# A second expert unit's first layer as seven block products instead of 32 plain ones, with the sums and counts around it moved

## The chip, the cores and the metric

The kernel runs on one core of one Trainium2 chip. The metric is the device time of one execution in microseconds (us). Three runs of the kernel before the change took 675.66, 675.84 and 678.24 us, median 675.84. One execution was profiled; it took 678.39 us, of which its instructions span 676.7 us.

The engines are named as in the profile: PE (matrix multiplication, with PEld for its weight loads), DVE (vector), ACT (scalar), POOL (GpSimd) and SP (the queue that issues most transfers). Each engine runs its own list of instructions strictly in order, and waits on semaphores for what other engines and transfers have not yet delivered.

## The reference

```python
# 1. attention, B=8, H=8, S=576, head_dim 64: causal, with a bias from a running sum of relu(s)
scores = scale * q @ k.T + minimum(-(cum_i - cum_j), 0)      # masked above the diagonal
x = softmax(scores) @ v                                      # -> x: (8, 576, 512)
# 2. a mixture of experts on x: E=8 experts, D=512, F=1024
logits = x @ w_gate
local_gate = sigmoid(x @ w_local)
e = argmax(logits) if s == 0 or local_gate < 0.5 else e of the token before
p = softmax(logits)
out = p[e] * (relu(x @ w1[e]) @ w2[e])                       # one expert per token, all float32
```

## The kernel before, in words

**Attention, then experts.** The attention runs batch by batch for the first 200 us. The tokens are routed in four groups of two batches: DVE finds each token's expert and its row in a table in memory, and POOL scatters the rows of `x` into this table (`put` in the class `Router`, L367 a memset and L370 an indirect transfer; 18 scatters a group, then 8 that store padding). The last group's routing and scatters overlap with the experts.

**Units.** The experts' work is cut into units, one letter each in `ORDER` (L66). Nearly all are whole units: up to 256 tokens of one expert. A unit has two layers: `x @ w1` with relu, and `h @ w2` with the gate. The phases alternate: (1,0), (1,1), (2,0), (1,2), (2,1), (1,3), (2,2) and so on, where (1,u) is the first layer of unit u and (2,u) its second. PE runs them in this order without a break between them.

**Plain and block layers.** A letter P in `ORDER` has a plain first layer (`layer1`, L864): 8 chunks of 4 products of 128x128 by 128x256, each of which the chip runs as two matmuls, so 64 matmuls. ACT alone turns the result into `hT` with a relu (L866). A letter D has its first layer, and both letters have their second layer, as seven block products in place of eight (`layer_split`, Winograd's form of Strassen's scheme): the tokens' matrix and the weights are each cut into 2x2 blocks, a11 to a22 and b11 to b22. Before the products come sums: `row_sums` makes s1 = a21+a22, s2 = s1-a11 and a21 = a11-a21 (L703 to L705), `row_fourth` a12 = a12-s2 (L709), and `weight_first` to `weight_fourth` make t1 = b12-b11, t2 = b22-t1, b12 = b22-b12 and b21 = b21-t2 (all L654). The order of the products is

- product 1 (a11, b11), copied by ACT to `sa`; product 2 (a12, b21), added to it by DVE as c11; then the fourth weight sum and the fourth row sum;
- product 6 (s2, t2), product 7 (a21, b12), product 5 (s1, t1), product 4 (a22, b21 after its sum), product 3 (a12 after its sum, b22).

After each, DVE adds the product to the partial sums (L762: c11, sb, sa, sb again and c22, c21, c12), and ACT applies the relu (L770) or the gate (L766). In the first layer a product is 16 matmuls of 128x128 by 128x128 (L730), in the second 8 of 128x128 by 128x256 (L737).

**Who does the sums.** DVE does all weight sums and, for the first five units, the row sums of `xT`; POOL does the row sums of `hT` for all units. The row sums of `hT` of unit 0 stand at the start of phase (1,1), those of unit 1 at the third step of (2,0).

**What sets the order.** The order is written out by hand. A layer calls `at(i)` after its i-th step; a table `todo`, filled by `plan` and `job`, says what is issued there on the other engines. `at` also takes the next waiting scatter, and lets it wait for the latest ACT instruction so far (`self.relu`): the scatters are spread over the steps, one a step. A plain layer has eight steps and a block layer seven. After all scatters and paddings are out, the rows of unit 5 and its `w1` may be loaded.

**Whole units assigned.** `assign_doubles` (its rows run from L387 to L465) computes with 26 small DVE instructions which expert and which rows the units 5 and later have. It needs the counts of the last group (`late_rows`, planned at step 2 of phase (1,1)).

## Time and profile before

| | |
|---|---|
| runs | 675.66, 675.84, 678.24 us; median 675.84 |
| profiled execution | 678.39 us, span 676.7 us, clock 0.996 |
| PE busy | 661.4 us (98%) |
| DVE busy | 492.9 us (73%) |
| POOL busy | 369.5 us (55%) |
| ACT busy | 195.5 us (29%) |
| phase (1,0), plain | from 200.46 us, with 1.5 us of routing in it |
| phase (2,0) starts | 230.37 us |
| phases (1,2), (2,1), (1,3), (2,2), (1,4) start | 242.45, 255.60, 267.69, 280.19, 292.28 us |

The shares are averages over the attention and the experts. Around the change, between 215 and 295 us, they are others, so the reader should look at stretches of time. In the timeline a row has the start in us, the length in us, the engine, line, operation, output and inputs, shapes, how many instructions are merged, and in brackets the idle time before and what ended it.

### The profile page before, as it was taken

Reading aid. Unit: us, or ns where it says so; the run is one execution under the profiler, and the core shown is the slowest. Engines: PE = TensorE matmul, PEld = TensorE weight load, DVE = VectorE, ACT = ScalarE, POOL = GpSimd, SP = SyncE. Lnnn points to the kernel's source line nnn. Section 1 sums busy time; section 2 is a strip of 40 time slices with the busy share of each in tenths; the row PEclk is TensorE's granted clock in tenths of the full one; section 3 lists DMA queues with packets and bytes.
Section 4 is the critical chain, followed back from the end, with each engine's and each line's share of the span. In section 5 each row is a group of like instructions: output and inputs, shape, how many; then the busy total and the mean of one; then the engine's idle time right before and its main releaser. Section 6 shows DMA issues by size and latency. Waiting matters only on the chain.

```text
span 676.7 us, 18439 instructions
## 1 busy us (share of the span) xinstructions
PE 661.4 (98%) x7501; PEld 571.4 (84%) x7501; DVE 492.9 (73%) x942; ACT 195.5 (29%) x353; POOL 369.5 (55%) x525
## 2 busy tenths in 40 slices
PE   8999999999999999999999999999999999999995
PEld 6888787888878899999999999999589687796884
DVE  4565857987966899978988988955467664766843
ACT  4454635546332112122122121212111121111111
POOL 3562377777645878955556557540642543714733
PEclk9999999999999999999999999999999999999998
DMA  7665575677549798489967455616939785933002
GB/s 263 193 176 167 177 219 177 213 228 245 181 129 398 227 341 266 191 275 346 349 262 254 182 188 187 253 44 248 353 58 392 277 364 130 291 144 115 25 15 76
DMA packets 56549, 145.75 MB, mean 215 GB/s; under 512 B 13104, under 2 KB 33968, under 8 KB 51464
## 3 DMA queue, kind: packets, MB, share of 16 engines
q1 hardware_dynamic: 47352, 124.23, 55.6%
q0 software_dynamic: 9008, 20.11, 8.3%
q8 instruction: 61, 1.00, 0.6%
q14 instruction: 32, 0.26, 0.1%
q10 hardware_dynamic: 96, 0.15, 0.1%
HBM read 123.83 MB, written 20.85 MB: 214 GB/s over the span
## 4 chain that ended last, share of the span: by engine, by line
PE 84%; DVE 7%; issue 4%; POOL 2%; DMA 1%; ACT 0%; SPq 0%; POOLq 0%; DVEq 0%
PE p L730 26%; PE p L737 25%; PE ps L1217 10%; PE po L1274 6%; PE pb L1274 6%; PE hp L864 3%; PE yp L887 2%; PE hp L855 2%; PE lp L237 1%; PE ph L1235 1%; POOL out_dram L839 1%; DVE wt L654 1%; PE po L1287 1%; DVE w2b L654 1%; PE pb L1287 1%
## 5 line engine op out<-in xcount | busy, mean ns | idle before, releaser
L737 PE MATMUL p<-w2b,hT 128*128 128x256 f32 (+1 forms) x720 | 163.0, 379 | 0.0
L737 PEld LDWEIGHTS p<-w2b,hT 128*128 128x128 f32 (+1 forms) x720 | 133.3, 187 | 21.9 <-PE hp L855 1.6
L730 PE MATMUL p<-xTs,w1b 128*128 128x128 f32 (+1 forms) x1040 | 142.9, 295 | 0.0
L730 PEld LDWEIGHTS p<-xTs,w1b 128*128 128x128 f32 x1040 | 137.9, 191 | 3.6 <-issue 1.6
L1218 ACT ACTIVATE e<-ps 128x768 f32<-128x768 f32 (+1 forms) x96 | 76.6, 885 | 60.9 <-PE ps L1217 60.8
L839 POOL DMA_INDIRECT out_dram<-y,gi x37 | 47.0, 1270 | 74.0 <-ACT y L766 66.2
L766 ACT ACTIVATE y<-y,gi 128x256 f32<-128x256 f32 (+1 forms) x71 | 34.5, 505 | 161.5 <-DVE y L762 161.5
L770 ACT ACTIVATE hT<-hT 128x512 f32<-128x512 f32 (+1 forms) x52 | 36.8, 711 | 143.8 <-DVE hT L762 143.8
L1217 PE MATMUL ps<-qb,kb 64*128 64x384 f32 (+4 forms) x516 | 76.8, 442 | 0.5 <-DVE xb L1297 0.4
L1217 PEld LDWEIGHTS ps<-qb,kb 64*128 64x128 f32 x516 | 47.5, 187 | 27.4 <-ACT e L1218 9.7
L370 POOL DMA_INDIRECT table<-xb,idx x54 | 56.8, 1052 | 14.2 <-issue 12.8
L737 PE MATMUL p<-wt,hSs 128*128 128x256 f32 (+1 forms) x272 | 63.3, 379 | 0.0
L709 POOL TENSOR_TENSOR hT<-hT,hSs 128x512 f32<-128x512 f32 (+1 forms) x14 | 21.1, 1506 | 76.8 <-PE p L737 76.7
L1201 POOL TENSOR_SCALAR_AFFINE_SELECT e<-e 128x128 f32<-128x128 f32 (+1 forms) x96 | 37.4, 406 | 41.8 <-ACT e L1218 41.0
L730 PE MATMUL p<-xSs,wt 128*128 128x128 f32 (+1 forms) x416 | 58.9, 295 | 0.4 <-DVE wt L654 0.4
L737 PEld LDWEIGHTS p<-wt,hSs 128*128 128x128 f32 (+1 forms) x272 | 50.7, 186 | 8.0
L730 PEld LDWEIGHTS p<-xSs,wt 128*128 128x128 f32 x416 | 55.6, 192 | 1.1 <-PE p L730 0.6
L762 DVE TENSOR_TENSOR hT<-p,sa 128x512 f32<-128x512 f32 (+1 forms) x48 | 31.2, 667 | 32.7 <-PE p L730 32.7
L1274 PE MATMUL pb<-vg,e 128*64 128x66 f32 x1280 | 41.4, 222 | 2.0 <-issue 1.9
L1274 PE MATMUL po<-vg,e 128*64 128x66 f32 x1280 | 41.4, 223 | 1.8 <-issue 1.8
L1274 PEld LDWEIGHTS pb<-vg,e 128*64 128x64 f32 x1280 | 39.4, 138 | 2.7 <-issue 2.6
L1274 PEld LDWEIGHTS po<-vg,e 128*64 128x64 f32 x1280 | 38.9, 138 | 3.3 <-issue 2.1
(304 smaller groups left out, 952.5 us busy)
## 6 DMA issues: line engine op xcount, KB each, us to landing
w2b<-in_w_dram SPq DMA_DIRECT2D x20, 2048.0 KB
w1b<-in_w_dram SPq DMA_DIRECT2D x19, 2048.0 KB
va<-in_v_dram SPq DMA_DIRECT2D x32, 320.0 KB
xq<-table SPq DMA_DIRECT2D x72, 130.0 KB
kb<-in_k_dram SPq DMA_DIRECT2D x31, 288.0 KB
qb<-in_q_dram SPq DMA_DIRECT2D x31, 288.0 KB
w1b<-in_w_dram SPq DMA_DIRECT2D x4, 512.0 KB
table<-xb,idx POOLq DMA_INDIRECT x54
```

The source lines that it names most:

```text
L370: put = self.nc.gpsimd.indirect_dma_start(out=self.halves, in_=src, element_offset=0, in_offset=None, out_offset=bass.IndirectOffsetOnAxis ...
L709: self.adder(u, layer).tensor_tensor(a12, a12, (self.xS, self.hS)[layer][u][1], op=Alu.subtract)
L730: mm(ps[:, m * h : m * h + h], lhsT=b[:, k, (c * of + m) * P : (c * of + m) * P + P], rhs=a[:, k, :], start=m == 0 and k == 0, stop=m == o ...
L737: mm(ps[:p, c * w : c * w + w], lhsT=a[:, k, c * p : c * p + p], rhs=b[:, k, :], start=c == 0 and k == 0, stop=c == parts - 1 and k == n - 1)
L762: nc.vector.tensor_tensor(to[:, c], part, s[:, c], op=Alu.add)
L766: ins = nc.scalar.mul(to[:, c], to[:, c], gi[:p, parts * r + c, 1:2]).ins
L770: return gated(to, r) if layer else nc.scalar.activation(to, to, Act.Relu).ins
L839: put = nc.gpsimd.indirect_dma_start(out=out, out_offset=bass.IndirectOffsetOnAxis(ap=idx, axis=0), in_=y, element_offset=0, bounds_check= ...
L1201: nc.gpsimd.affine_select(out=ap, in_=ap, compare_op=Alu.is_ge, fill=0.0, base=base, pattern=n, channel_multiplier=-1)
L1217: mm(ps[:, h, at : at + z - a], lhsT=kb[d, key : key + P], rhs=qb[d, a:z], start=True, stop=True)
L1218: exps[n, u] = nc.scalar.activation(e[:, :, : WIDTH[u]], ps, Act.Exp, scale=scale).ins
L1274: of = mm(po[part][d, j - a, :], lhsT=weights_of(n, c, j, h), rhs=vgs[n % NV][:, c if j < 2 * G1 else G1 + c, h, :], start=(first and i == ...
```

## The change

Unit 1 becomes a D: its first layer runs as seven block products. Its row sums of `x` and its three first weight sums are issued in phase (1,0), at steps 3 to 6. Phase (1,1) thereby has seven steps in place of eight. The three sums of the first unit's `w2` are issued one at each of steps 4, 5 and 6 of phase (1,1), ahead of the additions of that step's next product, where before they stood at its end. `assign_doubles` is no longer run at step 5 of phase (1,1): it is a generator with one more stop, taken piece by piece at steps 2 and 4 of (1,2), steps 1, 3 and 4 of (2,1), and step 0 of (1,3).

```diff
-ORDER = "PPDDDDDDDDXTXDMXD"
+ORDER = "PDDDDDDDDDXTXDMXD"
...
         v.tensor_scalar(x, x, float(REST_MIN), None, Alu.is_ge)
+        yield
         v.tensor_tensor(x, x, self.used, op=Alu.add)
...
-        plan(1, 1, 5, lambda: list(router.assign_doubles()))
+        doubles = router.assign_doubles()
+        for place in ((1, 2, 2), (1, 2, 4), (2, 1, 1), (2, 1, 3), (2, 1, 4), (1, 3, 0)):
+            plan(*place, lambda: next(doubles, None))
...
                     if u == 0:
-                        places = (1, 1, 6), (1, 1, 7), (1, 1, 7)
+                        places = (1, 1, 4), (1, 1, 5), (1, 1, 6)
...
-                    job(2, u - 2, 1 if self.kind(u - 2) in "DX" else "pre" if u > 2 else 3, self.row_sums, u, 0)
+                    elif u == 1:
+                        places = (1, 0, 4), (1, 0, 5), (1, 0, 6)
+                    if u == 1:
+                        job(1, 0, 3, self.row_sums, u, 0)
+                    else:
+                        job(2, u - 2, 1 if self.kind(u - 2) in "DX" else "pre" if u > 2 else 3, self.row_sums, u, 0)
```

Lines of the class `Experts` stand one further down in the changed kernel (L655 for L654, L763 for L762, L704 to L706 for L703 to L705).

On DVE, in phases (1,0) and (1,1), the scan `incl` that ends the last group's routing was followed at once by the group's rows (`at` and on):

```order
L314 SCALAR_TENSOR_TENSOR incl<-seg,hot 128x152
L331 TENSOR_TENSOR at<-pos,base 128x144
L333 TENSOR_TENSOR base<-base,pos 128x8
L334 TENSOR_TENSOR at<-at,hot 128x144
L336 TENSOR_REDUCE row<-at 128x18
```

Now there stand in the same place, from `incl` to the first row of the group:

```order
L314 SCALAR_TENSOR_TENSOR incl<-seg,hot 128x152
L704 TENSOR_TENSOR xSs<-xTs 128x256
L705 TENSOR_TENSOR xSs<-xSs,xTs 128x256
L706 TENSOR_TENSOR xTs<-xTs 128x2x128
L655 TENSOR_TENSOR wt_4100<-w1b 128x1024
L655 TENSOR_TENSOR wt_4100<-w1b,wt_4100 128x1024
L655 TENSOR_TENSOR w1b<-w1b 128x2x512
L763 TENSOR_TENSOR hT<-p_4167,sa 128x4x128
L655 TENSOR_TENSOR w1b<-w1b,wt_4100 128x2x512
L710 TENSOR_TENSOR xTs<-xTs,xSs 128x2x128
L763 TENSOR_TENSOR sb<-p_4187,sa 128x512
L331 TENSOR_TENSOR at<-pos,base 128x144
```

The row sums, weight sums and first additions of unit 1 have come ahead of the group's rows.

The next place on DVE is the end of phase (1,1) and the start of unit 0's second layer, (2,0). Before, `assign_doubles` ended there, and the sums of unit 0's `w2` followed it:

```order
L433 TENSOR_SCALAR bused<-bused 128x8
L434 TENSOR_TENSOR bused<-bused,n_f 128x8
L465 TENSOR_TENSOR a0used<-a0used,bused 128x8
L654 TENSOR_TENSOR wt_4269<-w2b 128x1024
L654 TENSOR_TENSOR wt_4269<-w2b,wt_4269 128x1024
L654 TENSOR_TENSOR w2b<-w2b 128x4x256
L762 TENSOR_TENSOR y<-p_4298,sa 128x256
```

Now the other additions of unit 1's first layer stand between the end of the group's rows (`pad_i`) and that place, with the sums of unit 0's `w2` among them:

```order
L381 TENSOR_SCALAR pad_i<-pad_at,half 128x8
L763 TENSOR_TENSOR sa<-p_4226,sb 128x512
L763 TENSOR_TENSOR sb<-p_4239,sb 128x512
L763 TENSOR_TENSOR hT<-p_4239,sa 128x4x128
L655 TENSOR_TENSOR wt_4251<-w2b 128x1024
L763 TENSOR_TENSOR hT<-p_4255,sa 128x4x128
L655 TENSOR_TENSOR wt_4251<-w2b,wt_4251 128x1024
L763 TENSOR_TENSOR hT<-p_4269,sb 128x4x128
L655 TENSOR_TENSOR w2b<-w2b 128x4x256
L763 TENSOR_TENSOR y<-p_4298,sa 128x256
```

All the parts of `assign_doubles` are gone from here; they stand among the additions of phases (1,2) and (2,1).

On POOL, at the end of phase (2,1), the stores of unit 1's output (`out_dram`) and the first paddings stood before in this order:

```order
L370 DMA table<-xb,idx 75264x260
L838 MEMSET gap 1x1
L839 DMA out_dram<-y,gi 4608x512
L367 MEMSET gap 1x1
L370 DMA table<-pad,pad_i 75264x260
L838 MEMSET gap 1x1
L839 DMA out_dram<-y,gi 4608x512
L367 MEMSET gap 1x1
L370 DMA table<-pad,pad_i 75264x260
L703 TENSOR_TENSOR hSs<-hT 128x512
```

and now:

```order
L840 DMA out_dram<-y,gi 4608x512
L367 MEMSET gap 1x1
L370 DMA table<-xb,idx 75264x260
L839 MEMSET gap 1x1
L840 DMA out_dram<-y,gi 4608x512
L367 MEMSET gap 1x1
L370 DMA table<-pad,pad_i 75264x260
L704 TENSOR_TENSOR hSs<-hT 128x512
```

Every scatter from step 7 of the old phase (1,1) on has moved one place back, since that phase has one step fewer: between the row sums of `hT` of unit 0 and its fourth row sum there are eight scatters in place of nine, and ahead of the fourth row sum of unit 2 there are seven paddings after unit 2's three row sums in place of six. The order on SP has not changed.

## The prediction

> **What bounds the kernel now.** I read the page first, for the share of each engine, then the timeline of PE around the change for its waits, and then a table of stretches, one for each phase from (2,0) on.
>
> ```profile
> PE 661.4 (98%) x7501; PEld 571.4 (84%) x7501; DVE 492.9 (73%) x942; ACT 195.5 (29%) x353; POOL 369.5 (55%) x525
> ...
> PE   8999999999999999999999999999999999999995
> ```
>
> PE is busy to the end, with no slice in which a delay could be lost again. What PE saves or waits between 200 and 300 us, the kernel saves or loses. Its rows there:
>
> ```profile
> 207.30 14.08 PE L864 MATMUL hp<-xTs,w1b 128*128 128x256 f32 x64
> 221.22 0.42 PE L322 MATMUL pos<-incl,first 128*128 128x152 f32 x2
> ...
> 221.73 8.80 PE L864 MATMUL hp<-xTs,w1b 128*128 128x256 f32 x40
> 230.37 3.62 PE L737 MATMUL p<-w2b,hT 128*128 128x256 f32 x16
> ...
> 242.45 3.73 PE L730 MATMUL p<-xTs,w1b 128*128 128x128 f32 x32
> 246.59 2.02 PE L730 MATMUL p<-xSs,wt 128*128 128x128 f32 x16 [0.40 <-DVE wt L654]
> ...
> 267.69 3.73 PE L730 MATMUL p<-xTs,w1b 128*128 128x128 f32 x32
> 280.19 3.62 PE L737 MATMUL p<-w2b,hT 128*128 128x256 f32 x16
> 288.82 3.62 PE L737 MATMUL p<-w2b,hT 128*128 128x256 f32 x16
> 292.28 3.73 PE L730 MATMUL p<-xTs,w1b 128*128 128x128 f32 x32
> ```
>
> The reader should see one wait in 80 us: 0.40 us at 246.59, for the second weight sum of unit 2. Every other sum came in time. By how much is seen from the engines that make the sums:
>
> ```profile
> 230.40:242.50 12.10, 12.10 (x58) 10.65 (x57) 11.90 (x14) 1.26 (x3) 10.49 (x11) 1.00 1.02 381
> 242.50:255.60 13.10, 12.70 (x114) 12.54 (x113) 13.00 (x18) 3.29 (x7) 10.03 (x16) 1.00 0.91 293
> 255.60:267.70 12.10, 12.10 (x59) 10.58 (x58) 11.93 (x16) 2.87 (x6) 10.29 (x17) 1.00 0.84 292
> 267.70:280.20 12.50, 12.50 (x114) 12.50 (x113) 10.43 (x13) 2.95 (x5) 10.99 (x14) 1.00 0.71 254
> ```
>
> The columns are length, PE, PEld, DVE, ACT, POOL, clock and transfers. DVE is full until 267.7 (11.90 of 12.10, 13.00 of 13.10, 11.93 of 12.10). POOL shows 10 to 11 us a phase, and most of the rest is the short gap between a scatter's memset and its transfer. Neither can take on work or make up lost time there.
>
> **The change part by part.** All sums are made against the profiled execution's clock; it took 678.39 us, 2.55 above the median of 675.84, and the difference found is put on the median.
>
> *PE, saved.* 64 plain matmuls take 221.22 - 207.30 = 13.92 us, seven block products of unit 3 280.19 - 267.69 = 12.50 us: **-1.4 us**. Unit 1's layer starts at 230.37 - 0.51 - 13.92 = 215.9 us (0.51 is the routing between 221.22 and 221.73) and its products take 12.50 / 7 = 1.79 us each.
>
> *DVE, added.* Seven additions of 0.68 (a row below has two in 1.28), four weight sums of 1.22, four row sums of 0.42: 11.3 us. The gap to hold them:
>
> ```profile
> 215.15 0.47 DVE L314 TENSOR_TENSOR_SCAN incl<-seg,hot 128x152 f32<-128x152 f32 x1
> 221.93 0.31 DVE L331 TENSOR_TENSOR at<-pos,base 128x144 f32<-128x144 f32 x1 [6.31 <-PE pos L323]
> 225.25 0.16 DVE L387 TENSOR_TENSOR cnt<-base,base 128x8 int32<-128x8 f32 x1
> 230.34 0.17 DVE L465 TENSOR_TENSOR a0used<-a0used,bused 128x8 f32<-128x8 f32 x1
> 230.43 1.27 DVE L654 TENSOR_TENSOR wt<-w2b 128x1024 f32<-128x1024 f32 x1
> 234.09 0.42 DVE L762 TENSOR_TENSOR y<-p,sa 128x256 f32<-128x256 f32 x1
> 234.43 4.17 DVE L654 TENSOR_TENSOR w2b<-w2b,wt 128x1024 f32<-128x1024 f32 x1
> 241.62 0.42 DVE L705 TENSOR_TENSOR xTs<-xTs 128x256 f32<-128x256 f32 x1
> 245.23 1.21 DVE L654 TENSOR_TENSOR wt<-w1b,wt 128x1024 f32<-128x1024 f32 x1
> 254.22 1.28 DVE L762 TENSOR_TENSOR hT<-p,sa 128x512 f32<-128x512 f32 x2
> ```
>
> 6.31 us were idle; `assign_doubles` (225.25 to 230.43, 5.2 us) leaves, which makes 11.5 us of room for 11.3 us. But the gap is not empty for the memory: POOL makes the row sums of `hT` of unit 0 in it.
>
> ```profile
> 218.43 1.28 POOL L703 TENSOR_TENSOR hSs<-hT 128x512 f32<-128x512 f32 x1
> 219.78 1.27 POOL L704 TENSOR_TENSOR hSs<-hSs,hT 128x512 f32<-128x512 f32 x1
> 221.01 1.27 POOL L705 TENSOR_TENSOR hT<-hT 128x512 f32<-128x512 f32 x1
> ...
> 235.02 1.28 POOL L709 TENSOR_TENSOR hT<-hT,hSs 128x512 f32<-128x512 f32 x1
> 236.24 1.27 POOL L703 TENSOR_TENSOR hSs<-hT 128x512 f32<-128x512 f32 x1
> 237.59 2.15 POOL L704 TENSOR_TENSOR hSs<-hSs,hT 128x512 f32<-128x512 f32 x1
> ...
> 287.93 1.03 POOL L370 DMA_INDIRECT table<-pad,pad_i  x1 [0.22 <-issue]
> 288.99 1.28 POOL L709 TENSOR_TENSOR hT<-hT,hSs 128x512 f32<-128x512 f32 x1
> ```
>
> With DVE idle each of POOL's sums takes 1.27 us. Where both engines sum, they take turns: DVE's sum at 234.43 takes 4.17 us in place of 1.22 while POOL runs two of its own, and then POOL's third takes 2.15, until DVE's is done.
>
> *First wait, product 6 of unit 1.* DVE is free at 215.6; row sums to 216.8, first weight sum to 218.0. The weights are there: PE multiplies with them from 215.9 on today. The second sum would be done at 219.2, in time for product 6 at 215.9 + 2 x 1.79 = 219.5. But POOL's first sum starts at 218.43. Bounds: no wait, or POOL's sum first, then 218.43 + 1.28 + 1.2 = 220.9 and product 6 at 221.1 (0.2 from DVE to PE, 246.44 to 246.59). I take the second, nearest to the 4.17 row, where DVE also began first: **+1.6**. [...]
>
> *Second wait, product 6 of (2,0).* Taking turns, the third weight sum ends at 223.3 and POOL's third sum at 224.5; then fourth weight and row sum and an addition to 226.7, the group's rows 3.3 (221.93 to 225.25) to 230.0, three additions to 231.9, first sum of `w2`, an addition and second sum to 234.9. PE: 221.1 + 5 x 1.79 + 0.51 = 230.55 end of layer, two products of 1.73 (288.82 to 292.28 is two), 234.0. It waits until 235.1: **+1.1** (0 to 2).
>
> *Third wait, product 6 of (1,2).* DVE adds and sums until 236.7; then comes the list that took 234.09 to 246.44 before, 12.35 us with POOL's sums of unit 1 in it, now as then: 249.05. PE: 235.1 + 5 x 1.73 + 2 x 1.79 = 247.3, starts 249.25: **+1.9**, where 0.4 was before. PE is now 249.25 - 246.59 = 2.7 us late. `assign_doubles` follows in pieces; the first two (15 of its 26 instructions, 3.0 us) come in (1,2). They are hidden only as long as DVE is not waited for: the fourth sum of (2,1) is; 0 to 2.8 us, which POOL's delay below covers.
>
> *POOL, the last wait.* The row that I hold to decide is the last one quoted. POOL's fourth row sum of unit 2 ends at 288.99 + 1.28 = 290.27, and product 3 that needs it starts at 288.82 + 1.73 = 290.55: 0.28 us to spare, behind 70 us of POOL work without a pause worth naming. A scatter that follows at once costs 1.27 us:
>
> ```profile
> 226.33 0.09 POOL L367 MEMSET gap<- 1x1 f32 x1
> 226.64 0.96 POOL L370 DMA_INDIRECT table<-xb,idx  x1 [0.22 <-issue]
> 227.60 0.09 POOL L367 MEMSET gap<- 1x1 f32 x1
> ...
> 254.94 1.23 ACT L770 ACTIVATE hT<-hT 128x512 f32<-128x512 f32 x2 [5.70 <-DVE hT L762]
> ```
>
> After 224.5 four scatters run to 229.6. The next is tied to the relu of c22, which ACT could do behind PE's plain chunks before and now does behind DVE: 231.9 + 0.6 (254.94: two in 1.23). It starts at 232.6 in place of 227.60; the two after it wait for the relus of c21 and c12 (234.3, 236.1). An eighth scatter, then the fourth row sum of unit 0 starts at 238.7 in place of 235.02: 3.7 late. To unit 2's the way is 288.99 - 235.02 = 54.0 us as before, plus the one scatter that moved behind (1.27): 5.0 late. In (1,2) the scatters again wait for relus; DVE's c22 (254.22) comes 2.6 + 1.5 later, so about 1 us more, up to 2.5 if c21 and c12 hold POOL too; a pause of 1.2 us on POOL that is there today may be used up against it. So POOL's sum is 6.0 us late (5.0 - 1.2 = 3.8 to 5.0 + 2.5 = 7.5), and product 3 of (2,2) starts 6.0 - 0.28 = **5.7 us late** (3.5 to 7.2). PE's own 2.7 lie inside, not on top. From there nothing gives it back. Sum: 675.84 + 5.7 = **681.5 us**.
>
> SP's order is as before. Unit 5's loads go when the last padding is stored, so they slip by as much as PE.
>
> **The rivals.**
>
> *Nothing blocks, and the layer is simply shorter.* If the sums of the two engines do not hold each other up in the gap, DVE is through at 220.4, POOL keeps its pace, all waits vanish, the 0.4 too: -1.4 - 0.4, 674.0 us, not slower. For it: the room of 11.5 us for 11.3. Against it: 4.17 and 2.15. It decides from the second weight sum on: if that ends by 219.4, this one is on.
>
> *POOL catches up.* The scatters tied to late relus lose their time in pauses that POOL has anyway. Then only DVE's three waits count: +2.7, 678.5 us. For it: 10 to 11 us busy of 12 to 13. Against it: the missing time is the gap inside each scatter.
>
> *DVE does not get free either.* The pieces of `assign_doubles` make the fourth sum of (2,1) 2.8 us late as well, unit 2's `hT` follows, and POOL's three sums of it wait: 5.7 + 2.8, 684.3 us. For it: at 261 us DVE and POOL meet again. Against it: DVE has 2 us to spare from 267.7 on.
>
> **How the numbers follow.** Forecast 0.62, its own range 679.3 to 683.0 us (3.5 to 7.2 late); DVE not free either 0.12; POOL catches up 0.13; nothing blocks 0.13. About 0.5%, 3.4 us, is what a measurement here can tell from no change. Slower by more: the forecast and the third rival, 0.74. Within: 0.24, the other two. Faster by more would take 3.4 us, and all that there is to gain is 1.8: 0.02, for what I have not seen. The range reaches down to 677.0, which takes in POOL's catching up, and up to 685.0, past the third rival.
>
> **What would show it.** In the changed kernel's timeline: seven products of about 12.5 us plus a wait in phase (1,1); the second sum of unit 1's `w1` longer than 2 us beside POOL's sums at 218 to 224; waits of PE for L655 at product 6 of (1,1), (2,0) and (1,2); scatters on POOL that wait for ACT's relus near 230 us; and a wait of some 3 us of PE for POOL's fourth row sum before product 3 of (2,2). No such last wait, and I am wrong about POOL; no wait at all in (1,1), and I am wrong about the two engines' sums.

## The result and the profile after

Three runs of the changed kernel took 687.52, 688.67 and 689.42 us, median **688.67**, against 675.84 before: ratio 1.0164, 95% interval 1.0137 to 1.0192. It is slower, as forecast, but above the range of 677.0 to 685.0. The profiled execution took 689.42 us with a span of 687.7, which is 11.0 more than the 676.7 of before. The medians differ by 12.8; the 1.8 between probably lie in the first number, since in four of the five later comparisons before had medians of 677.86, 678.17, 678.01 and 676.96.

The page of the changed kernel, its busy times, PE's slices and the clock granted to PE:

```profile
PE 665.9 (97%) x7549; PEld 575.9 (84%) x7549; DVE 506.0 (74%) x957; ACT 195.4 (28%) x350; POOL 372.6 (54%) x525
...
PE   8999999999999989979999999999999999999995
...
PEclk9999999999999999989999999999999999999998
```

PE has work of 1.4 us less and is yet busy 4.5 us longer. The slices show two gaps (the 15th and the 18th of 17.2 us each), and the clock has a dent at the second. The timeline of PE shows the places (start, length, engine, line, tiles, count, and in brackets the idle time before):

```profile
200.28 5.45 PE L865 MATMUL hp<-xTs,w1b 128*128 128x256 f32 x24
...
215.85 3.73 PE L731 MATMUL p<-xTs,w1b 128*128 128x128 f32 x32
...
228.87 3.62 PE L738 MATMUL p<-w2b,hT 128*128 128x256 f32 x16
233.85 1.96 PE L738 MATMUL p<-wt,hSs 128*128 128x256 f32 x8 [1.36 <-DVE wt L655]
...
242.56 3.73 PE L731 MATMUL p<-xTs,w1b 128*128 128x128 f32 x32
249.20 3.61 PE L731 MATMUL p<-xSs,wt 128*128 128x128 f32 x16 [2.90 <-DVE wt L655]
252.60 2.03 PE L731 MATMUL p<-xTs,w1b 128*128 128x128 f32 x16
...
293.06 1.89 PE L738 MATMUL p<-w2b,hT 128*128 128x256 f32 x8
298.73 3.78 PE L738 MATMUL p<-w2b,hT 128*128 128x256 f32 x8 [3.78 <-POOL gap L839]
302.30 4.53 PE L731 MATMUL p<-xTs,w1b 128*128 128x128 f32 x32
```

Phase (1,1) takes 13.02 us (215.85 to 228.87, with 0.51 of routing) where it took 14.4: the saving of 1.4 is there. Then come three waits: product 6 of (2,0), product 6 of (1,2), product 3 of (2,2). A second thing stands in the same rows. From start to start, the product behind the 2.90 us wait takes 3.40 us (249.20 to 252.60) in place of 1.79, the one behind the last wait 3.57 in place of 1.73, and the two after that 4.37 in place of 3.57. The table of stretches gives the reason (the last three columns are the granted clock, the transfers' share and GB/s; ahead of 249.20 and from 306.60 on the clock is 1.00):

```profile
249.20:252.60 3.40, 3.40 (x16) 3.40 (x17) 3.40 (x6) 1.61 (x3) 2.90 (x5) 0.52 0.96 281
...
298.70:302.30 3.60, 3.57 (x8) 2.83 (x9) 0.00 (x0) 0.00 (x0) 1.08 (x2) 0.50 0.43 118
302.30:306.60 4.30, 4.30 (x33) 4.29 (x32) 1.56 (x2) 1.10 (x2) 2.73 (x3) 0.81 0.86 223
```

After the two longer waits PE runs at half its clock for a while (0.52 and 0.50). The wait of 1.36 us and the 0.40 us wait of before had no such trail: the clock is 1.00 over the product behind each (233.80 to 235.70, and 246.60 to 248.40 in before), which takes 1.80 and 1.86 us. In the runs below, slow clock stands for the time by which the products behind a wait exceed their usual length; the granted clock itself was read here and in e6_waits.

On the engines that PE waits for, the gap in (1,1) first, DVE and then POOL:

```profile
217.73 1.23 DVE L655 TENSOR_TENSOR wt<-w1b,wt 128x1024 f32<-128x1024 f32 x1
...
238.81 3.01 DVE L704 TENSOR_TENSOR xSs<-xTs 128x256 f32<-128x256 f32 x1
```

```profile
218.57 1.51 POOL L704 TENSOR_TENSOR hSs<-hT 128x512 f32<-128x512 f32 x1
...
231.62 0.09 POOL L367 MEMSET gap<- 1x1 f32 x1 [1.74 <-ACT hT L771]
232.31 0.96 POOL L370 DMA_INDIRECT table<-xb,idx  x1 [0.60 <-issue]
...
239.03 1.27 POOL L710 TENSOR_TENSOR hT<-hT,hSs 128x512 f32<-128x512 f32 x1
...
266.96 1.28 POOL L710 TENSOR_TENSOR hT<-hT,hSs 128x512 f32<-128x512 f32 x1
...
273.39 0.09 POOL L367 MEMSET gap<- 1x1 f32 x1 [1.40 <-ACT y L767]
...
297.41 1.27 POOL L710 TENSOR_TENSOR hT<-hT,hSs 128x512 f32<-128x512 f32 x1
```

The second weight sum of unit 1 was done before POOL's first sum mattered. DVE is then busy almost without a pause (12.78 us of 215.80 to 228.90, 16.96 of 228.90 to 246.10), with the sums of `w2` behind the group's rows. On POOL the three fourth row sums (L710) of units 0, 1 and 2 start at 239.03, 266.96 and 297.41; before they started at 235.02, 261.64 and 288.99.

**One yardstick for all runs.** The attention ahead of the change varies from execution to execution: phase (1,0) starts between 196.99 and 201.71 us in nearly all the traces below. So each profiled run is judged by its *rest*, the span less the start of phase (1,0). Before it is 676.7 - 200.46 = 476.2 us, after 687.7 - 200.28 = 487.4, which is **+11.2**. It comes from one execution of each kernel. Leaving out e14 to e17 it differs by up to 1.7 us from the difference of the medians, in e8_all_moved by 3.4; so a difference of a microsecond in it says little.

### The profile page after: what moved, and what is told of

Same layout as the page of the kernel before. It is cut to its first block, busy times and chain, and to the rows that moved or that the text cites. A ratio compares the mean times of both kernels' runs of the same rounds, so it can differ in the third digit from the quotient of the medians.

```text
span 687.7 us, 18548 instructions
## 1 busy us (share of the span) xinstructions
PE 665.9 (97%) x7549; PEld 575.9 (84%) x7549; DVE 506.0 (74%) x957; ACT 195.4 (28%) x350; POOL 372.6 (54%) x525
## 3 DMA queue, kind: packets, MB, share of 16 engines
q8 instruction: 62, 1.02, 0.6%
## 4 chain that ended last, share of the span: by engine, by line
PE 48%; POOL 6%; DVE 5%; issue 4%; ACT 0%; POOLq 0%; DVEq 0%
PE p L731 22%; PE p L738 22%; PE yp L888 2%; PE hp L856 2%; POOL table L370 2%; POOL out_dram L840 2%; DVE wt L655 1%; DVE w1b L655 1%; POOL hT L710 1%; POOL hT L706 1%; DVE sb L763 0%; DVE hT L763 0%; DVE g_good L1470 0%; POOL hSs L705 0%; DVE bstep L418 0%
## 5 line engine op out<-in xcount | busy, mean ns | idle before, releaser
L738 PE MATMUL p<-w2b,hT 128*128 128x256 f32 (+1 forms) x720 | 165.1, 382 | 3.8 <-POOL gap L839 3.8
L731 PE MATMUL p<-xTs,w1b 128*128 128x128 f32 (+1 forms) x1120 | 153.2, 294 | 0.0
L731 PEld LDWEIGHTS p<-xTs,w1b 128*128 128x128 f32 x1120 | 148.3, 193 | 3.8 <-issue 1.6
L771 ACT ACTIVATE hT<-hT 128x512 f32<-128x512 f32 (+1 forms) x56 | 39.4, 705 | 158.0 <-DVE hT L763 158.0
L370 POOL DMA_INDIRECT table<-xb,idx x54 | 58.8, 1088 | 15.7 <-issue 13.2
L731 PE MATMUL p<-xSs,wt 128*128 128x128 f32 (+1 forms) x448 | 64.3, 298 | 2.9 <-DVE wt L655 2.9
L731 PEld LDWEIGHTS p<-xSs,wt 128*128 128x128 f32 x448 | 60.8, 196 | 3.6 <-issue 3.1
L710 POOL TENSOR_TENSOR hT<-hT,hSs 128x512 f32<-128x512 f32 (+1 forms) x14 | 21.1, 1507 | 77.1 <-PE p L738 77.1
L763 DVE TENSOR_TENSOR hT<-p,sa 128x512 f32<-128x512 f32 (+1 forms) x51 | 33.5, 668 | 32.4 <-PE p L731 29.9
```

The source lines that it names most:

```text
L370: put = self.nc.gpsimd.indirect_dma_start(out=self.halves, in_=src, element_offset=0, in_offset=None, out_offset=bass.IndirectOffsetOnAxis ...
L710: self.adder(u, layer).tensor_tensor(a12, a12, (self.xS, self.hS)[layer][u][1], op=Alu.subtract)
L731: mm(ps[:, m * h : m * h + h], lhsT=b[:, k, (c * of + m) * P : (c * of + m) * P + P], rhs=a[:, k, :], start=m == 0 and k == 0, stop=m == o ...
L738: mm(ps[:p, c * w : c * w + w], lhsT=a[:, k, c * p : c * p + p], rhs=b[:, k, :], start=c == 0 and k == 0, stop=c == parts - 1 and k == n - 1)
L763: nc.vector.tensor_tensor(to[:, c], part, s[:, c], op=Alu.add)
L771: return gated(to, r) if layer else nc.scalar.activation(to, to, Act.Relu).ins
```

## The experiments

"Now" means the changed kernel; diffs are against it unless another is named. The last column is the rest against the 476.2 us of before. In five of the six comparisons before had a median of 675.84 to 678.17 us. In the one of e14 to e17 it had 691.65, so their times are read by ratio and by the waits in their traces alone; of e16 the profiled execution (2089.55 us, three times the others) is not used.

| run | median, range (us) | ratio, 95% interval | rest |
|---|---|---|---|
| after | 688.67 (687.52 to 689.42) | 1.0164 (1.0137 to 1.0192) | +11.2 |
| e1_fill | 686.03 (684.82 to 687.21) | 1.0109 (1.0074 to 1.0144) | +8.8 |
| e2_unpaced | 685.31 (683.99 to 687.21) | 1.0106 (1.0068 to 1.0144) | +8.3 |
| e3_sums_later | 688.50 (686.75 to 688.84) | 1.0137 (1.0103 to 1.0171) | +9.7 |
| e4_plain | 681.34 (680.36 to 683.57) | 1.0048 (1.0028 to 1.0067) | +4.3 |
| e5_only_blocks | 684.92 (684.01 to 686.54) | 1.0106 (1.0082 to 1.0131) | +7.8 |
| e8_all_moved | 688.31 (687.09 to 690.45) | 1.0147 (1.0115 to 1.0179) | +13.5 |
| e9_assign_13 | 688.64 (688.45 to 690.58) | 1.0162 (1.0138 to 1.0187) | +11.6 |
| e10_whole | 684.54 (683.15 to 686.97) | 1.0118 (1.0083 to 1.0154) | +8.2 |
| e11_slack | 683.54 (682.39 to 686.74) | 1.0086 (1.0054 to 1.0118) | +7.0 |
| e12_slack_w2 | 683.24 (679.26 to 684.56) | 1.0076 (1.0055 to 1.0097) | +5.9 |
| e13_slack_plain | 682.65 (680.80 to 684.95) | 1.0086 (1.0059 to 1.0112) | +3.9 |
| e14_untied | 705.75 (702.61 to 708.07) | 1.0218 (1.0181 to 1.0254) | +5.4 |
| e15_untied_later | 705.68 (705.28 to 705.82) | 1.0203 (1.0174 to 1.0233) | +5.7 |
| e16_untied_plain | 704.07 (701.62 to 704.58, without the profiled one) | 1.0173 (1.0137 to 1.0209) | |
| e17_untied_as_now | 705.70 (704.39 to 708.25) | 1.0218 (1.0183 to 1.0253) | +5.1 |
| e18_room | 680.06 (677.67 to 681.46) | 1.0042 (1.0026 to 1.0058) | +2.0 |
| e19_room_plain | 679.60 (678.06 to 683.01) | 1.0039 (1.0020 to 1.0058) | +2.5 |

### The slow products behind the waits

Small matmuls whose result nobody reads are put where PE waited, so that it does not stand idle.

```diff
+        def fill(n):
+            ps = self.bank("fill")[:, :P]
+            for _ in range(n):
+                nc.tensor.matmul(ps, lhsT=router.ones, rhs=router.ones, start=True, stop=True)
+        plan(1, 2, 1, lambda: fill(12))
+        plan(2, 2, 5, lambda: fill(16))
```

> The changed kernel with matmuls that nobody uses put on PE in the two places where it waited longest: 12 products of 128x128 ahead of product 6 of (1,2), 16 ahead of product 3 of (2,2). What they compute is thrown away. Theory 1 (after an idle stretch of some 3 us PE is given half the clock for some 3 us): product 6 of (1,2) takes 1.8 us again and not 3.4, product 3 of (2,2) 1.7 and not 3.6, the two after it 3.6 and not 4.4. If POOL's sum still comes when it came, the 1.6 us at the first place only lengthen the last wait, and 2.6 us are saved: 686.1 us; if POOL comes earlier too, up to 4.4: 684.3. Rival (the products are slow because their operands or the memory are slow): the same rows stay slow, 688.7 us or more.

It took 686.03 us, rest 2.4 less than after. PE's rows at the last wait, in this run:

```profile
292.28 3.73 PE L982 MATMUL fill<-r_ones 128*128 128x128 f32 x32
297.49 1.99 PE L738 MATMUL p<-w2b,hT 128*128 128x256 f32 x8 [1.47 <-POOL gap L839]
299.32 3.73 PE L731 MATMUL p<-xTs,w1b 128*128 128x128 f32 x32
```

PE is held up as long as before, since POOL's sum ends where it did; but the product behind it takes 1.83 us (297.49 to 299.32) in place of 3.57, and the one at (1,2) 1.86. The slow clock behind the last wait, 1.84 + 0.80 = 2.64 us, is gone, and 2.4 of it shows in the rest. The slow clock at (1,2), 1.61 us, returned nearly nothing: product 3 of (2,2) starts 297.49 - 199.35 = 98.1 us after (1,0), against 298.73 - 200.28 = 98.5 in the changed kernel. There POOL is what PE waits for, and PE's own lateness lies inside its wait.

How long a wait may be was measured in the kernel before: chains of copies on ACT, of 7, 10, 13, 16, 20 and 26, hold back one short matmul ahead of product 6 in each of six phases, (1,4) to (1,9). The diff is against the kernel before.

```diff
+WAITS = {4: 7, 5: 10, 6: 13, 7: 16, 8: 20, 9: 26}
...
+                if what == 1 and u in WAITS and i == 0:
+                    for _ in range(WAITS[u]):
+                        nc.scalar.copy(scr, scr)
+                if what == 1 and u in WAITS and i == 1:
+                    nc.tensor.matmul(self.bank("late")[:, :P], lhsT=router.ones, rhs=scr[:, :P], start=True, stop=True)
...
+        scr = router.first
```

> The kernel before, with a wait of PE of a chosen length put into each of the phases (1,4) to (1,9), ahead of product 6: one small matmul there needs the end of a chain of 7, 10, 13, 16, 20 or 26 copies of 128x128 on ACT (thrown away). Waits of about 1, 2, 3, 4, 5 and 6.5 us are expected, estimated from 0.3 us a copy. Theory 1 (the clock falls to half after an idle stretch and comes back after some 3.4 us): no slow product behind waits up to 1.8 us, 1.5 to 1.8 us lost behind each of 2.4 us or more, and not more behind the long ones. Rival (the loss grows with the wait, or comes from late operands): nothing lost behind these waits, or more behind the longer.

It took 707.1 us, in a single execution. Three of the six places in PE's timeline:

```profile
320.19 0.49 PE L1057 MATMUL late<-first,r_ones 128*128 128x128 f32 x2 [2.11 <-ACT first L1055]
320.52 1.95 PE L731 MATMUL p<-xSs,wt 128*128 128x128 f32 x16
322.31 1.95 PE L731 MATMUL p<-xTs,w1b 128*128 128x128 f32 x16
...
348.37 0.49 PE L1057 MATMUL late<-first,r_ones 128*128 128x128 f32 x2 [3.09 <-ACT first L1055]
348.70 2.92 PE L731 MATMUL p<-xSs,wt 128*128 128x128 f32 x16
351.40 2.66 PE L731 MATMUL p<-xTs,w1b 128*128 128x128 f32 x16
...
445.17 0.79 PE L1057 MATMUL late<-first,r_ones 128*128 128x128 f32 x2 [7.38 <-ACT first L1055]
445.76 3.24 PE L731 MATMUL p<-xSs,wt 128*128 128x128 f32 x16
448.83 1.95 PE L731 MATMUL p<-xTs,w1b 128*128 128x128 f32 x16
```

After idle times of 1.12 and 2.11 us the products keep their 1.79, at a clock of 1.00. After 3.09, 4.08, 5.40 and 7.38 us the next two lose 1.6, 1.6, 1.2 and 1.3 us together. The clock granted to these two is 0.64 and 0.70, 0.63 and 0.73, 0.58 and 1.00, 0.56 and 1.00. So in this run the loss did not grow with the wait.

### Each part of the change alone

Without the block products: `ORDER` as before, the sums of `w2` and the assignment as now.

```diff
-ORDER = "PDDDDDDDDDXTXDMXD"
+ORDER = "PPDDDDDDDDXTXDMXD"
```

> The changed kernel with unit 1 left plain: only the sums of the first w2 at steps 4 to 6 and the assignment in pieces are new. Theory 1 (the loss comes from the block layer's work on DVE; moving the assignment alone costs nothing): within 1 us of the kernel before, 675 to 677 us. Rival (the pieces of the assignment in (1,2) and (2,1) are what DVE lacks time for): PE waits in (1,2) to (2,2), 678 us or more.

It is slower than before by 0.48% and by 4.3 us in the rest. One new wait makes that up:

```profile
260.97 1.89 PE L738 MATMUL p<-wt,hSs 128*128 128x256 f32 x8
265.14 5.38 PE L738 MATMUL p<-w2b,hT 128*128 128x256 f32 x16 [2.29 <-DVE bstep L415]
270.36 3.73 PE L731 MATMUL p<-xTs,w1b 128*128 128x128 f32 x32
```

In (2,1) product 4 comes 2.44 us late, and it and product 3 take 5.22 in place of 3.45, 1.77 more. What is late is the fourth weight sum of (2,1), just ahead of `bstep` on DVE: the pieces of the assignment in (1,2) pushed it back to 262.02 us, beside POOL's sums, and it took 2.97 us.

Only the block products: the assignment and the sums of `w2` where they were.

```diff
-        for place in ((1, 2, 2), (1, 2, 4), (2, 1, 1), (2, 1, 3), (2, 1, 4), (1, 3, 0)):
-            plan(*place, lambda: next(doubles, None))
+        plan(1, 1, 5, lambda: list(doubles))
...
-                        places = (1, 1, 4), (1, 1, 5), (1, 1, 6)
+                        places = (1, 1, 6), (1, 1, 7), (1, 1, 7)
```

> The changed kernel with the other two edits undone: the assignment runs whole at step 5 of (1,1) again, and the three sums of the first w2 stand at the end of (1,1), behind its last additions. Only the block layer itself is new. Theory 1 (DVE's room is what lacks, 11.3 us of new work and 5.2 us of assignment against 6.3 us idle; each PE wait beyond some 2 us costs 1.7 us of clock more): the wait before product 6 of (2,0) grows from 1.5 to 6 us or more, with a clock loss; 690 to 694 us. Rival (the assignment in pieces is worse than whole): faster than the changed kernel, 684 to 687 us.

It took 684.92 us, where I had expected 690 to 694: 3.4 us less in the rest than the whole change, as the rival had it. There is one wait, 7.20 us, and the two products behind it lose 1.82 and 0.46:

```profile
237.54 3.75 PE L738 MATMUL p<-wt,hSs 128*128 128x256 f32 x8 [7.20 <-DVE wt L655]
241.09 2.35 PE L738 MATMUL p<-w2b,hT 128*128 128x256 f32 x8
```

So the two edits that make room for the block products do not help them: +7.8 for the blocks alone, +4.3 for the edits alone, +11.2 together.

The assignment alone put back, the sums of `w2` as now:

```diff
-        for place in ((1, 2, 2), (1, 2, 4), (2, 1, 1), (2, 1, 3), (2, 1, 4), (1, 3, 0)):
-            plan(*place, lambda: next(doubles, None))
+        plan(1, 1, 5, lambda: list(doubles))
```

> The changed kernel with the assignment of whole units back where it was, in one run at step 5 of phase (1,1); the block products and the sums of w2 ahead stay. Against the run with the block products alone (684.9 us, one wait of 7.4 us at product 6 of (2,0)) only the place of the sums differs. Theory 1, DVE has no room in the gap and the 5.2 us of the assignment go straight into that wait: a wait of 6.7 us (1.5 + 5.2) and about 1.7 of slow clock, no wait of 2.3 us or more later, 684 us (682.5 to 686). Rival, it was the late place of the sums that made the wait of 7.4: the wait is under 4 us and the time under 682.

684.54 us, as the first theory had it:

```profile
235.74 3.75 PE L738 MATMUL p<-wt,hSs 128*128 128x256 f32 x8 [6.53 <-DVE wt L655]
```

Between the starts of two products PE loses 6.70 us, 5.1 more than the 1.6 that the run shares with the changed kernel, which is the 5.2 us of the assignment. The early sums of `w2` shorten the wait by 0.7 us (7.37 to 6.70), but the rest no further (+8.2 against +7.8), since 0.74 us are then waited in (1,2). Set against now, it is better to pay for the assignment once, at +8.2, than to spread it, at +11.2.

### Moving single pieces of work

The scatters of (1,1) and (1,2) are no longer tied to ACT's relus.

```diff
-                    self.puts.pop(0)(self.relu)
+                    self.puts.pop(0)(None if (what, u) in ((1, 1), (1, 2)) else self.relu)
```

> The changed kernel, but the scatters taken in phases (1,1) and (1,2) no longer wait for the latest ACT instruction. The order on POOL stays. Theory 1 (POOL came late at unit 2's fourth row sum because its scatters were tied to relus that DVE made late): POOL's waits for ACT of some 5 us between 215 and 275 us are gone, its sum starts at 293 to 295 us and not 297.4, the last wait of PE falls from 3.9 us below 1.5, without the clock loss behind it: 682 to 684 us. Rival (POOL is late because it and DVE take turns at the memory, the ties only fill its queue): its sum starts within 1 us of 297.4, 688 us.

Rest 2.9 us less than after. POOL's fourth row sum of unit 2 comes 1.6 us sooner (293.65 - 198.12 = 95.5 us after the start of (1,0), against 97.1). PE arrives sooner too, since its wait in (1,2) fell to 1.63 us, with no slow product behind it; so its last wait is as long as ever:

```profile
245.83 2.02 PE L731 MATMUL p<-xSs,wt 128*128 128x128 f32 x16 [1.63 <-DVE wt L655]
...
294.98 2.70 PE L738 MATMUL p<-w2b,hT 128*128 128x256 f32 x8 [3.77 <-POOL gap L839]
```

The row sums of unit 1's `hT` on POOL come a phase later, away from DVE's row sums of unit 2.

```diff
-                        place = ((1, 1, "pre"), (2, 0, 2))[u]
+                        place = ((1, 1, "pre"), (1, 2, 0))[u]
```

> The changed kernel, but POOL's three row sums of unit 1's hT are issued at step 0 of (1,2) and no longer at step 2 of (2,0), so that they do not run beside DVE's row sums of unit 2. Theory 1 (taking turns with POOL made DVE's three row sums last from 238.8 to 244.6, 5.8 us in place of 1.3): the wait of PE before product 6 of (1,2) falls from 3.1 us to nearly 0, and its clock loss of 1.6 with it; POOL's late sum of unit 2 then takes most of this back, so 684 to 688 us. Rival (DVE is simply overloaded): the wait stays above 2 us, 688.7 us.

The wait in (1,2) is gone: it was POOL's sums beside DVE's. But a wait of 2.34 us for the fourth weight sum of (2,1) comes in its place, with 1.76 us of slow clock. By the starts this is 4.3 us, which gives back most of the 4.7 that the wait in (1,2) and its slow clock had cost. The last wait (3.78) stays, with 1.75 us of slow clock behind it in place of 2.64. The rest is 1.5 us less, the medians are alike.

The assignment is spread over (1,3) instead; in the second of these runs three more things are moved.

```diff
-        for place in ((1, 2, 2), (1, 2, 4), (2, 1, 1), (2, 1, 3), (2, 1, 4), (1, 3, 0)):
+        for place in ((1, 3, 1), (1, 3, 2), (1, 3, 3), (1, 3, 4), (1, 3, 5), (1, 3, 6)):
```

> The changed kernel with one edit altered: the assignment's pieces stand at steps 1 to 6 of (1,3) in place of (1,2) and (2,1). Theory 1 (the two waits in (2,0) and (1,2) come ahead of the pieces and stay; DVE's relus in (1,2) come 3 us earlier, so POOL's scatters tied to them too): POOL's fourth row sum of unit 2 some 2 us earlier, the last wait of PE 2 us and not 3.9: 684 to 687 us. Rival (the pieces do not matter beside the block layer): 688.7 us.

Beside this, in the second: the sums of `w2` at step 1 of (1,1), POOL's sums a phase later, and the scatters two a step in (1,0) and untied up to (1,2).

```diff
-                        places = (1, 1, 4), (1, 1, 5), (1, 1, 6)
+                        places = ((1, 1, 1),) * 3
-                        place = ((1, 1, "pre"), (2, 0, 2))[u]
+                        place = ((1, 1, "pre"), (1, 2, 0))[u]
-                    self.puts.pop(0)(self.relu)
+                    for _ in range(2 if not now and len(self.puts) > 1 else 1):
+                        self.puts.pop(0)(self.relu if now > 3 else None)
```

> The changed kernel with each of its waits attacked at its cause: the assignment in pieces all in (1,3), behind the fourth sum of (2,1); the three sums of the first w2 at step 1 of (1,1), ahead of the group's rows on DVE; POOL's row sums of unit 1's hT at step 0 of (1,2); two scatters a step in (1,0), and no scatter tied to an ACT instruction before phase (2,1). Theory 1 (the block layer saves 1.4 us, and all else were waits of PE and the clock lost behind them): no PE wait above 1 us between 215 and 305 us, 1 to 2 us faster than the kernel before of the same call. Rival (there is more work than DVE and POOL can do in these 80 us, in any order): waits elsewhere, 3 us or more slower than the kernel before.

Neither was faster: 688.64 and 688.31 us. In the first POOL's fourth row sum of unit 2 comes 1.9 us sooner (294.21 - 198.97 = 95.2 us after the start of (1,0)), and PE no longer waits for it in (2,2); it waits longer for DVE one product ahead, whose fourth weight sum the pieces have pushed back:

```profile
296.73 5.25 PE L738 MATMUL p<-w2b,hT 128*128 128x256 f32 x16 [4.76 <-DVE w2b L655]
```

The second has this wait too (4.69), and waits of 1.66 us in (1,1) and 2.30 in (2,1).

### Moving several at once

The pieces of the assignment go where DVE had waited for PE, the scatters of (1,1) and (1,2) are untied, POOL's sums come later, and (1,3) issues three paddings fewer.

```diff
-        for place in ((1, 2, 2), (1, 2, 4), (2, 1, 1), (2, 1, 3), (2, 1, 4), (1, 3, 0)):
+        for place in ((2, 1, 5), (1, 3, 0), (1, 3, 0), (1, 3, 0), (2, 2, 4), (2, 2, 5)):
...
-                        place = ((1, 1, "pre"), (2, 0, 2))[u]
+                        place = ((1, 1, "pre"), (1, 2, 0))[u]
...
-                if self.puts and (now, i) != (0, 2) and (now != 2 or i % 2 == 0):
-                    self.puts.pop(0)(self.relu)
+                if self.puts and (now, i) != (0, 2) and (now not in (2, 5) or i % 2 == 0):
+                    self.puts.pop(0)(None if (what, u) in ((1, 1), (1, 2)) else self.relu)
```

> The changed kernel with four things moved: the pieces of the assignment go where DVE waited for PE before (the last step of (2,1), step 0 of (1,3), the last steps of (2,2)); the scatters in (1,1) and (1,2) are not tied to ACT; POOL's row sums of unit 1 come at step 0 of (1,2); in (1,3) a padding is issued only at every second step, so three fewer stand ahead of POOL's fourth row sum of unit 2. Theory 1, the waits are what these queues make them, and half clock follows only waits over 2.3 us: the 1.6 us at product 6 of (2,0) stays, no wait over 2 us is left, 675 to 678 us. Rival, DVE has no room for the pieces anywhere in these phases: a wait of over 2.4 us comes back at a fourth weight sum of (2,1) or (2,2), with 1.7 us of slow clock, 680 us or more.

683.54 us, where I had expected 675 to 678. The waits for POOL are down to 1.37 and 1.09 us, without a trail, but one for a fourth weight sum comes up in (2,3), where the changed kernel has none, with 1.77 us of slow clock. Here are PE and DVE of this run:

```profile
320.13 5.16 PE L738 MATMUL p<-w2b,hT 128*128 128x256 f32 x15 [2.59 <-DVE w2b L655]
```

```profile
314.24 1.22 DVE L655 TENSOR_TENSOR wt<-w1b 128x1024 f32<-128x1024 f32 x1 [5.44 <-DMA w1b<-in_w_dram]
```

DVE had stood still for 5.44 us, for unit 5's weights. With the last pieces in (2,2), which expert unit 5 has was known too late, and SP fetched unit 6's rows ahead of these weights. This fault is in the next two runs as well. With the sums of `w2` at step 2 of (1,1), behind the last group's rows:

```diff
-                        places = (1, 1, 4), (1, 1, 5), (1, 1, 6)
+                        places = ((1, 1, 2),) * 3
```

> The run before this one with the three sums of unit 0's w2 moved again, from steps 4 to 6 to step 2 of (1,1), right behind the last group's rows. Theory 1, the wait at product 6 of (2,0) is DVE's queue alone: it goes, 1.6 us less than the run before, 674 to 676.5 us. Rival, the 3.6 us of sums only hold up the additions and relus behind them, and with them POOL or PSUM: a wait of at least 1 us comes in (1,1), (2,0) or (2,1), and the time is not below that of the run before.

The wait at product 6 of (2,0) is gone, as DVE's queue would have it. 0.77 us come back at product 4 of that phase, and POOL's fourth row sum of (2,1) is waited for 0.9 us longer. The medians are alike, the rest falls by 1.1: the expected time was missed. And the same with unit 1 plain:

```diff
-ORDER = "PDDDDDDDDDXTXDMXD"
+ORDER = "PPDDDDDDDDXTXDMXD"
```

> The run before this one with unit 1 plain again: only the block products are taken out. Theory 1, where nothing waits they are worth what PE saves, 1.4 us: 1.4 us slower than the run before (0.4 to 2.4). Rival, DVE's 11 us of added work in (1,0) and (1,1) still cost more than PE saves: this one is faster than the run before by 1 us or more.

The rest is 2.0 us shorter without the block products, the median 0.6; the intervals overlap. That seemed to say that the block products cost more than they save in any surroundings. The last pair below, without the fault on SP, does not bear it out.

No scatter tied at all, the pieces so that SP's order stays, and three kernels beside it: POOL's sums a phase later, unit 1 plain, and the pieces where the changed kernel has them.

```diff
-                    self.puts.pop(0)(self.relu)
+                    self.puts.pop(0)(None)
...
-                        places = (1, 1, 4), (1, 1, 5), (1, 1, 6)
+                        places = ((1, 1, 2),) * 3
...
-        for place in ((1, 2, 2), (1, 2, 4), (2, 1, 1), (2, 1, 3), (2, 1, 4), (1, 3, 0)):
+        for place in ((2, 1, 5), (1, 3, 0), (1, 3, 0), (1, 3, 0), (1, 3, 5), (1, 3, 6)):
```

> The changed kernel with no scatter or padding tied to ACT, the three sums of unit 0's w2 at step 2 of (1,1), and the assignment in pieces at the last step of (2,1) (one), step 0 of (1,3) (three) and the last two steps of (1,3), so that the order on SP is that of the changed kernel again: in the runs with pieces in (2,2), unit 6's rows were fetched ahead of unit 5's weights, and DVE waited 4 to 5 us for these at 310 us. Theory 1, with POOL's pauses and that late load gone only short waits are left, 1 to 2 us in (1,2) where DVE and POOL sum together, under 1 elsewhere: rest of the program +0 to +2 us against before, 676 to 680 us. Rival, DVE has more to do than it has idle time: waits of 3 us or more in all, one of them over 2.3 with its slow clock, rest +4 or more, 682 us or more.

> The run before this one with POOL's row sums of unit 1 at step 0 of (1,2). Theory 1, POOL has room once nothing ties its scatters: the wait in (1,2) goes and POOL's fourth row sum in (2,1) comes in time; at most the same time as the run before, and up to 1.6 us less. Rival, the sums only change their place in POOL's queue, and its fourth row sum of unit 1 is late in (2,1) by 1.4 to 2.5 us as in the two runs with pieces in (2,2): the same time or slower.

> The run two before this one with unit 1 plain: only the block products are taken out. Theory 1, with the queues in order the block products are worth what PE saves: this one is 0.5 to 1.5 us slower than that run. Rival, DVE's 11.3 us of added work show up as waits in any order: this one is faster than that run by 1 us or more, as it was by 2.0 in the rest of the program in the last pair.

> The changed kernel with two edits alone: no scatter or padding tied to ACT, and the sums of unit 0's w2 at step 2 of (1,1); the pieces of the assignment stay where the changed kernel has them. Theory 1, POOL's pauses made the last wait: it falls from 3.8 us to under 1.5 and no slow clock follows; the pieces in (1,2), uncovered, then make the fourth weight sum of (2,1) 1 to 2.5 us late, with up to 1.8 of slow clock: rest +3 to +6, 680 to 682.5 us. Rival, POOL is late by the scatters' own length, not by their pauses: the last wait stays at 3 us or more, rest +8, 684 us or more.

All four are slower than any run above, by ratio: 1.0173 to 1.0218. Phase (1,0) starts at 218.89, 221.77 and 221.01 us in the three traces, so some 20 us went before the change's place. I had freed the scatters of (1,0) too, which run beside the last of the attention; how much of the 20 us is theirs, and how much is what made before take 691.65 us here, no trace tells. In time these runs are inconclusive. By their waits: in e14 four, of 0.20, 1.66, 0.64 and 2.01 us, all for DVE and none for POOL; in e15 2.29 and 3.55 for POOL, so that POOL's sums are late again when they come later; in e17 the last wait fell from 3.78 to 2.07 us without a trail, and 2.14 came at (2,1), for the pieces that it had covered. Neither wait of e15 has slow products behind it, not even the one of 3.55 us, whose product takes 1.83 us (317.20 to 319.03):

```profile
317.20 1.99 PE L738 MATMUL p<-w2b,hT 128*128 128x256 f32 x8 [3.55 <-POOL gap L839]
319.03 3.73 PE L731 MATMUL p<-xTs,w1b 128*128 128x128 f32 x32
```

The runs e17 and e14 differ only in the places of the pieces. POOL's rows in e17, a store of `y` in (1,3) and the fourth row sum of unit 2, and that sum in e14:

```profile
294.27 1.18 POOL L840 DMA_INDIRECT out_dram<-y,gi  x1 [2.46 <-ACT y L767]
...
314.92 1.27 POOL L710 TENSOR_TENSOR hT<-hT,hSs 128x512 f32<-128x512 f32 x1
```

```profile
308.56 1.28 POOL L710 TENSOR_TENSOR hT<-hT,hSs 128x512 f32<-128x512 f32 x1
```

By the start of (1,0) the sum comes at 93.9 us in e17 and at 89.7 in e14, where POOL's first store of unit 1's `y` waits 0.23 us. So with no scatter tied, the pieces in (1,2) and (2,1) still make POOL 4.2 us later.

The same again with the scatters of (1,0) tied, and its pair without the block products.

```diff
-                    self.puts.pop(0)(self.relu)
+                    self.puts.pop(0)(None if now else self.relu)
```

> The changed kernel with the scatters tied to ACT in (1,0) alone, where the attention still runs, and free from (1,1) on; the sums of unit 0's w2 at step 2 of (1,1); the assignment in pieces at the last step of (2,1), step 0 of (1,3) (three) and the last two steps of (1,3), which leaves SP's order as it is. Theory 2, DVE has 11.3 us more to do than before and lacks about 5 us of idle time, so PE's waits for DVE add up to 4 to 6 us between (1,1) and (1,4), with none over 2.3 us and so hardly any slow clock: rest of the program +3 to +5.5 us, ratio 1.004 to 1.008. Theory 1, it was the order of the queues: waits under 2 us in all, rest +1.5 or less, ratio under 1.003.

> The run before this one with unit 1 plain: only the block products are taken out. Theory 2: DVE then has its 6 us of idle time in (1,1) again, the waits fall to 2 us or less in all, and this one is 1 to 3 us faster than the run before in the rest of the program. Theory 1: PE's saving of 1.4 us is all that differs, and this one is 0.5 to 1.5 us slower.

680.06 us, ratio 1.0042, and of the 11.2 us in the rest 2.0 are left. PE's two waits in (2,0) and (1,2) and POOL's fourth row sums of units 0 and 2 in this run:

```profile
237.32 3.69 PE L738 MATMUL p<-w2b,hT 128*128 128x256 f32 x16 [1.97 <-DVE w2b L655]
...
245.16 2.02 PE L731 MATMUL p<-xSs,wt 128*128 128x128 f32 x16 [0.58 <-DVE wt L655]
```

```profile
233.59 1.28 POOL L710 TENSOR_TENSOR hT<-hT,hSs 128x512 f32<-128x512 f32 x1
...
288.30 1.27 POOL L710 TENSOR_TENSOR hT<-hT,hSs 128x512 f32<-128x512 f32 x1
```

There is no wait for POOL any more, and the longest, of 1.97 us, has no slow clock behind it: the two products take 3.53 us together, where 3.45 is usual. By the start of (1,0) at 197.96, POOL's last sum starts at 90.3 us: 1.8 later than before (88.5), where the changed kernel had 97.1. What is left are waits for DVE, 2.12 and 0.74 us by PE's starts and 0.4 behind them. The plain half takes 679.60 us; its rest is 0.5 us *longer*, and phase (1,4) starts 94.07 us after (1,0) in place of 93.50. So in these two traces the block products give 0.5 of their 1.4 us; the medians cannot tell the two apart. Neither theory is borne out whole. The order of the queues and the places of the pieces made most of the loss, 9 of 11.2 us; but the plain half is slower than before too (1.0039), by a wait of 1.67 us for the fourth weight sum of (2,2): the assignment, which cost nothing in its old place, costs some 1.8 us in the new ones. No kernel here is faster than the one before.

## Why the prediction was wrong

The direction held, and so did the chain of waits from the second on, with POOL's as the one that decides. The first wait did not come; the sum had no term for the clock, and its term for POOL's lateness was too small.

- **PE, saved: -1.4.** Measured -1.4 (13.02 with 0.51 of routing against 13.92 + 0.51).
- **First wait, +1.6: wrong.** It is 0, the other of my two bounds. The row is of the kind of the 4.17 us: on POOL a scatter ran straight into the sum, and DVE's row had begun ahead of that sum, there by 0.59 us, here by 0.84 (217.73 against 218.57, where I had reckoned 218.0 against 218.43). With this lead DVE's sum took its usual 1.23 us, and POOL's took 1.51 in place of 1.28. In the run with all moved POOL's first sum began 0.08 us ahead of DVE's (214.35 against 214.43) and DVE's took 2.29 in place of 1.2. The sign that I had set for the rival that nothing blocks, a second sum done by 219.4, came true (218.96), and yet the third took 2.29 us beside POOL's.
- **Second wait, +1.1:** measured 1.5. **Third, +1.9 where 0.4 was:** measured 3.1. The errors cancel: I had PE 2.7 us late at product 6 of (1,2), due at 249.25; it started at 249.20.
- **The clock, no term: the first step that failed.** I went on from 249.25 with products of 1.79 us. The first took 3.40, at a granted clock of 0.52. The same after the last wait cost 2.64 us at the end, where nothing covers it. The dummy matmuls gave 2.4 of it back. The trace of before could not have shown it, since its only wait there was 0.40 us. The traces of the runs have 1.2 to 1.8 us after most waits from 2.29 us up, 2.3 to 2.8 after four and nothing after three: a wait of 2.29 us already cost 1.77 (e4_plain), and one of 3.55 us nothing (e15_untied_later).
- **POOL, 6.0 late: the second, a term mis-sized.** The three scatters behind c22, c21 and c12 began with their memsets at 231.62, 233.35 and 235.09, a microsecond sooner than predicted (232.6, 234.3, 236.1); the third's transfer took 1.90 us, and the fourth row sum of unit 0 came at 239.03 (predicted 238.7). But from there to unit 2's I counted one scatter and 1 to 2.5 us of pauses, less a pause of 1.2 that was to be used up. By the start of (1,0), the three sums are 4.2, 5.5 and 8.6 us late: 4.4 more on the way, of which the scatter is 1.3 and the pauses, old against new, 3.1. Of the old pause 0.8 was used up (0.44 us at 245.97, before 1.23 at 243.37). But POOL stood for 1.02 and 0.33 us for relus at 259.45 and 261.43, and for 1.40 us at 273.39 for `y`, ahead of unit 2's row sums. Untying the scatters of (1,1) and (1,2) took 1.6 us off.
- **Product 3 of (2,2), 5.7 late:** by the start of (1,0) it is 98.45 - 90.09 = 8.4 late.
- **"PE's own 2.7 lie inside, not on top" and "from there nothing gives it back":** both held. The 1.6 us of slow clock in (1,2) lay inside as well.
- **The pieces of the assignment, 0 to 2.8 at the fourth sum of (2,1), covered by POOL's delay:** as a wait of PE they were covered in the changed kernel. Uncovered, in the run without the block products, they cost 2.44 us, and 1.77 of clock behind it. But they also delay POOL, for which the sum had no more than the pauses of (1,2). In that same run POOL's fourth row sum of unit 0 comes in time (34.50 us after the start of (1,0), before 34.56) and that of unit 2 is 4.2 us late (92.75 against 88.53), PE's new wait included; the changed kernel loses 4.4 on the same way.

The miss of 688.67 - 681.5 = 7.2 us is thus 2.6 of clock at the end, 2.7 of POOL, 0.2 left over in the rest, and 1.6 by which the execution profiled stood closer to the one of before than the medians (11.2 against 12.8).

Of the rivals, that nothing blocks was right only in that PE did not wait in (1,1). POOL did not catch up. That DVE does not get free either did not happen in the changed kernel, but in the runs that took POOL's delay away. What I had not done for either engine was to follow its work to where it went: I counted the room in the gap (11.5 us for 11.3) as made by the assignment's leaving, and gave its 5.2 us one place in the sum, under POOL's delay.

**What made the loss.** The last wait was POOL's, with the slow clock behind it, and POOL's 8.6 us have two halves. The first 4.2, up to unit 0's fourth row sum, are mostly the ties. With the scatters free from (1,1) on (e18_room) this sum starts 35.63 us after (1,0), in place of 38.75; with the sums of `w2` at the same place but the scatters of (2,0) still tied (e12_slack_w2) it is 38.71. The other 4.4 hold the one scatter (1.3) and, in good part, the pieces of the assignment in (1,2) and (2,1): these cost POOL 4.2 without the block products, and 4.2 with no scatter tied, PE's own wait in (2,1) included. With ties and pieces both changed (e18_room) the last sum came 6.8 us sooner, and the long waits and their slow clock went. One thing alone gave less: 1.6 the ties of (1,1) and (1,2), 1.9 the pieces moved into (1,3) (e9_assign_13). So the division is near, not exact.

## What to carry to other kernels

When a change frees room on an engine by moving work elsewhere, look for room at the place it goes to as well, and follow every issue that is tied to the work which becomes later: here a few scatters tied to relus carried a delay of 4 us into another engine's queue, and the work moved elsewhere helped it to grow to 8.6. A wait of PE can cost more than its length: of the 20 waits here of 2.29 us or more, 17 cost another 1.2 to 2.8 us of slow clock, and on the path that sets the end this decides. When one wait is taken away, look at the next in line before counting the gain, since PE arrives there sooner; and when a wait appears where none was, look first whether the order of the loads has changed.
